# A transformer block on one core: the epsilon of both norms as a third triple of the statistics, negated means left out, and the waits of an instruction put in another order

## The chip, the cores and the metric

The kernel runs on one core of one Trainium2 chip. The metric is the device time of one execution in microseconds; of the kernel before, three runs took 204.25, 204.28 and 204.39 us, the median is 204.28 us. Lines such as L515 are lines of the kernel before, unless the text says otherwise.

## The reference

One layer: a norm, an attention with softmax feature maps and linear cost, a residual; then a second norm, a gated feed-forward part and a residual. S is 2048 rows, D 448, 16 heads of 28, F 1792, all in bf16.

```python
def _layernorm(x, axis=-1, eps=1e-5):
    m = jnp.mean(x, axis=axis, keepdims=True)
    v = jnp.var(x, axis=axis, keepdims=True)
    return (x - m) / jnp.sqrt(v + eps)

def _A_ref(x, wqkv, w_phi, wo):
    qkv = (x @ wqkv).reshape(B, S, 3, H, Dh).transpose(2, 0, 3, 1, 4)
    q, k, v = qkv[0], qkv[1], qkv[2]
    pq = jnp.einsum("bhsd,hdf->bhsf", q, w_phi)
    pk = jnp.einsum("bhsd,hdf->bhsf", k, w_phi)
    phi_q = jnp.concatenate([_softmax(pq), _softmax(-pq)], axis=-1)
    phi_k = jnp.concatenate([_softmax(pk), _softmax(-pk)], axis=-1)
    kv = jnp.einsum("bhsf,bhsd->bhfd", phi_k, v)
    z = jnp.einsum("bhsf->bhf", phi_k)
    num = jnp.einsum("bhqf,bhfd->bhqd", phi_q, kv)
    den = jnp.einsum("bhqf,bhf->bhq", phi_q, z)[..., None] + 1e-6
    return (num / den).transpose(0, 2, 1, 3).reshape(B, S, D) @ wo

h = x + _A_ref(_layernorm(x), A_wqkv, A_w_phi, A_wo)
ln = _layernorm(h)
h2 = h + (sigmoid(ln @ w_gate) * (ln @ w_up)) @ w_down
```

## The kernel before

The 2048 rows are 16 tiles of 128 rows, each a row of `x_sb` with 448 columns. Every piece of work is an operation with a name, such as `xn3` (the normalised rows of tile 3) or `kva5`. A table at the head of the file, `ORDER`, gives for each of the five engines the names in the order in which that engine runs them; for some operations it also decides on which engine they run, where the code offers two or three. The class `Graph` takes the operations with what they read and write, finds from that which must wait for which, and emits for every engine its queue with the waits. An engine runs its queue in order, so an instruction that waits holds back all behind it.

**The first norm.** For each tile `stats` records `bst` (`bn_stats`, six numbers a row: two triples of count, mean and sum of squared deviations) and `agg` (`bn_aggr`, which makes mean and variance of the triples, into `mv1`), both on VectorE. For groups of tiles (0, 1, 2 and 3 alone, 4-5, 6-7, 8 to 11, 12 to 15) `rstd` then records four operations, named after the first tile of the group: `ve1` adds epsilon to the variance (L522), `pow1` raises it to -1/2 on GpSimd (L527, into `rst1`), `nm1` negates the mean (L525), and `nb1` multiplies the negated mean by `rst1` (L531, from tile 2 on). `xnorm` makes the normalised tile `xn`: on ScalarE as scale times x plus bias (`rst1` and `nb1`, L540), on VectorE or GpSimd as (x + nm1) times rst1 (L543). There are three buffers for these tiles, so `xn7` can start when the transpose of tile 4 has read its buffer.

**From the normalised tile to the features.** Tiles 0 to 3 are transposed on TensorE (`xT0` to `xT3`, L507) and copied to `xnT` on ScalarE or VectorE (`xT0e` and so on, L500); from tile 4 on the transposes `xT` are DMAs from the SP queue, in order, with the load of the last two tiles of x (`x14`) between `xT5` and `xT6`. TensorE multiplies with the folded weights for k and phi (`pp` for two tiles, `pva`/`pvb` for one) and with those for v (`vv`, or the same pair). All matmuls of this kind work on 64 rows at a time, in two halves that run side by side and share line L305. ScalarE takes the exponentials of both signs (`ek`, L641 and L642), VectorE sums them (`ss`, L645) and takes the reciprocal (`rs`, L651), GpSimd or VectorE multiplies the two (`phi`, L655), and TensorE adds each tile to the sums over all rows with `kvb` and `kva`, whose operand is `phi` and v. Between these run the products for q (`pqa`, `pqb`), whose exponentials `eq` (L691) ScalarE takes.

**The second part.** `num` multiplies the features of q with the sums; VectorE forms `rsm`, `qq`, `b`, `c` and `rden` per tile (L768 to L776; the first two tiles share `rsm0` and `qq0`, L740 and L741), `o` is the attention's output (L780), `wo` the projection. For tiles 0 and 1 the residual is added by TensorE itself, and the second norm takes `bs2` (L799) and `ag2` (L802) from the result; `ve0` and `ve1` (L803) add epsilon, `pow2` (L817) raises, `hn` (L821) normalises with the mean as it stands. All other tiles of the second norm use sums of squares by ScalarE (`sq`) and keep their own `ve`. Then `ga`, `gb` (gate and up), `sig` (L881), `hh` (L882), `dn`/`dp`/`dm` (down), `fin` (L916) and the stores.

**The waits.** For each operation `emit` gathers what it has to wait for in `o.waits`, at most one entry per engine and one per DMA, sorted by the number under which the producer was recorded, highest first. The queue then issues one wait after another in that order. In the built program the last of them belongs to the instruction that follows; each earlier one, sometimes two together, is an instruction of its own.

Of the kernel before, what the change touches and what calls it, by code (L numbers as in the profile page):

```python
# [6 lines left out]
ALU = mybir.AluOpType  # L7
# [3 lines left out]
ENGINES = ("sp", "act", "pe", "dve", "pool")  # L11
# [7 lines left out]
class Graph:  # L19
# [86 lines left out]
    def emit(self, nc):  # L106
        ops = self.ops
        self.schedule()
        queues = {e: [] for e in ENGINES}
        for i in self.order:  # L110
            o = ops[i]
            o.pos = len(queues[o.eng])
            queues[o.eng].append(o)
        known = {e: {} for e in ENGINES}
        for i in self.order:
            o = ops[i]
            kn = known[o.eng]
            todo = []
            for j, raw in o.deps.items():
                p = ops[j]  # L120
                if self.needs_wait(p, o, raw):
                    key, v = (("d",) + p.sem, p.val) if p.dma is not None else (("e", p.eng), p.pos + 1)
                    todo.append((key, v, j))
            todo.sort(key=lambda t: -t[2])
            o.waits = []
            for key, v, j in todo:
                if kn.get(key, 0) >= v:
                    continue
                o.waits.append(j)
# [58 lines left out]
P = 128  # L188
D = 448
# [10 lines left out]
EPS = 1e-5  # L200
# [57 lines left out]
    ),  # L258
    "dve": (
# [16 lines left out]
    ),  # L276
    "pool": (
# [5 lines left out]
    ),  # L283
# [38 lines left out]
def build(nc, A_x, A_wqkv, A_w_phi, A_wo, B_w_gate, B_w_up, B_w_down, out):  # L322
    S = A_x.shape[1]
    assert A_x.shape[0] == 1 and A_x.shape[2] == D and S == 2048
    NT = S // P
# [7 lines left out]
    with ExitStack() as es:  # L333
        def sb(name, shape, d=dt.bfloat16):
            return es.enter_context(nc.sbuf_tensor(name, shape, d))
        f32 = dt.float32
# [2 lines left out]
        neghalf = sb("neghalf", [P, 4], f32)  # L339
        mask2 = sb("mask2", [P, 2], f32)  # L340
        par = sb("par", [P, 2])
        st2 = sb("st2", [P, 2, 6], f32)
        mv2 = sb("mv2", [P, 2, 2], f32)
        x_sb = sb("x_sb", [P, NT, D])
        h_sb = x_sb
        st1 = sb("st1", [P, NT, 6], f32)
        mv1 = sb("mv1", [P, NT, 2], f32)
        ve1 = sb("ve1", [P, NT], f32)
        rst1 = sb("rst1", [P, NT], f32)
        nb1 = sb("nb1", [P, NT], f32)  # L350
        nm1 = sb("nm1", [P, NT], f32)
        sum2 = sb("sum2", [P, NT], f32)
        nm2 = sb("nm2", [P, NT], f32)
        ssq2 = sb("ssq2", [P, NT], f32)
# [37 lines left out]
        def bk(i):  # L392
            return psum[:, i * 512:(i + 1) * 512]
# [9 lines left out]
        def B(i):  # L403
            return ("bank", i)

        def load(name, dst, src, w, kb, r=(), eng="sp"):
# [8 lines left out]
                                                      base=0, pattern=[[-1, P]], channel_multiplier=1),  # L415
           r=["ident"], w=["ident"])
        op("pool", "neghalf", lambda e: e.memset(neghalf[:], -0.5), w=["neghalf"])
        def epsl0(e):
            e.memset(epsl[:, 0:64], EPL)
            return e.memset(epsl[:, 64:P], 0.0)  # L420
# [90 lines left out]


        def stats(t):
            op("dve", "bst%d" % t, lambda e: e.bn_stats(st1[:, t, :], x_sb[:, t, :]), r=[("x", t)], w=[("st1", t)])  # L514
            op("dve", "agg%d" % t, lambda e: e.bn_aggr(mv1[:, t, :], st1[:, t, :]), r=[("st1", t)], w=[("mv1", t)])  # L515

        def rstd(ts):
            a, b = ts[0], ts[-1] + 1
            n = b - a

            def fve(e):
                return e.tensor_scalar(ve1[:, a:b], mv1[:, a:b, 1], EPS, None, op0=ALU.add)  # L522

            def fnm(e):
                return e.tensor_scalar(nm1[:, a:b], mv1[:, a:b, 0], -1.0, None, op0=ALU.mult)  # L525
            op(("dve", "pool"), "ve1_%d" % a, fve, r=[("mv1", t) for t in ts], w=[("ve1", a)])
            op("pool", "pow1_%d" % a, lambda e: e.tensor_tensor(rst1[:, a:b], ve1[:, a:b], neghalf[:, 0:n], ALU.pow),  # L527
               r=[("ve1", a), "neghalf"], w=[("rst1", a)])
            op(("dve", "pool"), "nm1_%d" % a, fnm, r=[("mv1", t) for t in ts], w=[("nm1", a)])
            if a >= 2:  # L530
                op("pool", "nb1_%d" % a, lambda e: e.tensor_tensor(nb1[:, a:b], nm1[:, a:b], rst1[:, a:b], ALU.mult),  # L531
                   r=[("nm1", a), ("rst1", a)], w=[("nb1", a)])

        def xnorm(t, a):
            s = t % NX
            src = windows(x_sb[:, t, :])
            dst = xn_pad[:, s, :].rearrange("p (a f) -> p a f", a=2)

            def fa(e):
                return e.activation(dst, src, ACT.Identity, bias=nb1[:, t:t + 1], scale=rst1[:, t:t + 1])  # L540

            def fd(e):
                return e.tensor_scalar(dst, src, nm1[:, t:t + 1], rst1[:, t:t + 1], op0=ALU.add, op1=ALU.mult)  # L543
            r = [("x", t), ("nm1", a), ("rst1", a)]
            if a < 2:
                op(("dve", "pool"), "xn%d" % t, fd, r=r, w=[("xn", s)])
            else:
                op(("act", "dve", "pool"), "xn%d" % t, (fa, fd, fd), r=r + [("nb1", a)], w=[("xn", s)])
            if t < 4:
                pe_transpose("xT%d" % t, [xn_pad[:, s, kt * P:(kt + 1) * P] for kt in range(KT)], 6 + t % 2,  # L550
                             xnT[0][:, :, TS(t)], ("xn", s), ("xnT", t))
            else:
                op("sp", "xT%d" % t, lambda e: e.dma_start_transpose(out=xnT[t // 4][:, :, TS(t)], in_=xn_pad[:, s, :]),
                   r=[("xn", s)], w=[("xnT", t)], dma="tr", nring=64)
# [241 lines left out]
        def resid(t, b, ha=False):  # L796
            c, s = t // 4, t % NH
            if ha:
                st = op("dve", "bs2_%d" % t, lambda e: e.bn_stats(st2[:, t % 2, :], bk(b)[:, 0:D]), r=[B(b)], w=[("st2", t)])  # L799
                op(("act", "dve"), "h%d" % t, (lambda e: e.copy(h_sb[:, t, :], bk(b)[:, 0:D]),  # L800
                                               lambda e: e.tensor_copy(h_sb[:, t, :], bk(b)[:, 0:D])), r=[B(b)], w=[("x", t)], after=[st])
                op("dve", "ag2_%d" % t, lambda e: e.bn_aggr(mv2[:, t % 2, :], st2[:, t % 2, :]), r=[("st2", t)], w=[("mv2", t)])  # L802
                op(("dve", "pool"), "ve%d" % t, lambda e: e.tensor_scalar(ve2[:, t:t + 1], mv2[:, t % 2, 1:2], 1.0, EPS, op0=ALU.mult,  # L803
                                                                          op1=ALU.add), r=[("mv2", t)], w=[("ve2", t)])
            else:
                op("dve", "h%d" % t, lambda e: e.scalar_tensor_tensor(out=h_sb[:, t, :], in0=bk(b)[:, 0:D], scalar=1.0, in1=x_sb[:, t, :],  # L806
                                                                      op0=ALU.mult, op1=ALU.add, accum_out=sum2[:, t:t + 1]),
                   r=[B(b), ("x", t)], w=[("x", t), ("sum2", t)])
            if not ha:
# [7 lines left out]
            op("pool", "pow2_%d" % t, lambda e: e.tensor_tensor(rst2[:, t:t + 1], ve2[:, t:t + 1], neghalf[:, 0:1], ALU.pow),  # L817
               r=[("ve2", t), "neghalf"], w=[("rst2", t)])
# [169 lines left out]
```

## Time and profile before

The profile is of one execution on the chip.

| what | value |
|---|---|
| median of three runs | 204.28 us |
| span of the profiled execution | 202.8 us |
| PE (matmuls) busy | 195.9 us, 97% of the span |
| VectorE (DVE) busy | 135.5 us, 67% |
| ScalarE (ACT) busy | 95.7 us, 47% |
| GpSimd (POOL) busy | 55.6 us, 27% |
| bn_aggr, L515, 16 times | 161 ns mean |
| ve1 / nm1 of one tile on POOL, L522 / L525 | 218 / 234 ns mean |
| pow1 of 1, 2 and 4 tiles, L527 | 571, 707 and 1006 ns mean |
| granted TensorE clock | 1.00 in every stage |

The time of a run is longer than the span, since it holds what lies before the first and behind the last instruction that the profile counts. Rows of the timeline give the start, the length, the engine and line, and in brackets how long the engine was idle before and what ended that. Busy times of PE are modelled ends of pipelined matmuls. An engine's share of the whole span is a mean over stages with different limits.

### The profile page before, as it was taken

What the parts mean: (1) busy time and instruction counts of PE and PEld (TensorE: products, weight loads), DVE (VectorE), ACT (ScalarE), POOL (GpSimd) and SP (SyncE); (2) the same over time, 40 slices, a digit from 0 to 9 for tenths busy, and PEclk for the clock granted to TensorE, in tenths of its full rate; (3) what the DMA queues carried; (4) which work ended last, traced back from release to release, by engine and by line L of the source; (5) the groups of instructions that cost most, each with busy time, mean ns of one, the idle gap of its engine ahead of it and who ended that gap; (6) DMA issues with size and microseconds to landing.
All of it is one profiled execution on the core that took longest, in us unless ns stands there. A gap on an engine that the chain in (4) does not pass through costs nothing.

```text
span 202.8 us, 5881 instructions
## 1 busy us (share of the span) xinstructions
PE 195.9 (97%) x2508; PEld 109.4 (54%) x2508; DVE 135.5 (67%) x328; ACT 95.7 (47%) x191; POOL 55.6 (27%) x97
## 2 busy tenths in 40 slices
PE   7889999999979999999999999999999999999995
PEld 3734556665448776677444444444554555454443
DVE  5899999979998897858667967536432422272224
ACT  3887989988882527222333342324422212222220
POOL 5599699723144303700033020001400000000000
DMA  6985516849949411251004411030212000004003
GB/s 154 316 141 123 80 33 89 230 158 279 308 37 229 55 31 29 50 82 26 3 3 100 100 29 26 3 74 24 58 47 54 0 0 3 0 3 136 0 0 94
DMA packets 32867, 16.27 MB, mean 80 GB/s; under 512 B 25096, under 2 KB 31944, under 8 KB 32840
## 3 DMA queue, kind: packets, MB, share of 16 engines
q1 hardware_dynamic: 32336, 15.86, 34.9%
q8 instruction: 20, 0.33, 0.7%
q10 hardware_dynamic: 504, 0.03, 0.2%
q14 instruction: 7, 0.06, 0.1%
HBM read 8.34 MB, written 1.84 MB: 50 GB/s over the span
## 4 chain that ended last, share of the span: by engine, by line
PE 84%; DVE 8%; POOL 2%; DMA 2%; issue 1%; SPq 1%; ACT 0%; DVEq 0%
PE psum L305 78%; PE psum L909 5%; DVE st L514 2%; DMA x_sb<-in_A_x_dram 2%; DVE ss L645 2%; POOL o_pad L780 1%; DVE b_sb L771 1%; DVE xn_pad L543 1%; SPq L407 1%; DVE c_sb L774 1%; PE psum L507 0%; POOL xn_pad L543 0%; DVE rs L651 0%; DVE xnT L500 0%; POOL rst L527 0%
## 5 line engine op out<-in xcount | busy, mean ns | idle before, releaser
L305 PE MATMUL psum<-xnT,wg_sb 64*128 64x512 bf16 (+1 forms) x490 | 93.1, 334 | 0.3 <-DVE rden L776 0.2
L305 PE MATMUL psum<-xnT,wu_sb 64*128 64x512 bf16 (+1 forms) x490 | 92.9, 334 | 0.0
L881 ACT ACTIVATE sg_sb<-psum 128x512 bf16<-128x512 f32 (+1 forms) x70 | 34.8, 511 | 91.4 <-PE psum L305 90.9
L882 DVE SCALAR_TENSOR_TENSOR hhT<-sg_sb,psum 128x512 bf16<-128x512 bf16 (+1 forms) x70 | 38.9, 576 | 53.3 <-ACT sg_sb L881 53.0
L305 PEld LDWEIGHTS psum<-xnT,wg_sb 64*128 64x128 bf16 x490 | 44.4, 94 | 23.4 <-DVE hhT L882 4.8
L305 PEld LDWEIGHTS psum<-xnT,wu_sb 64*128 64x128 bf16 x490 | 44.4, 94 | 13.5
L305 PE MATMUL psum<-wd_sb,hhT 64*128 64x448 bf16 x336 | 36.8, 350 | 0.0
L305 PEld LDWEIGHTS psum<-wd_sb,hhT 64*128 64x128 bf16 x336 | 16.9, 94 | 15.1 <-DVE x_sb L806 0.5
L305 PE MATMUL psum<-Wk,xnT 64*128 64x448 bf16 x112 | 22.1, 351 | 0.3 <-ACT Wk L500 0.2
L305 PE MATMUL psum<-wv_sb,xnT 64*128 64x448 bf16 x112 | 22.2, 351 | 0.1
L815 POOL TENSOR_SCALAR ve<-ssq 128x1 f32<-128x1 f32 x11 | 2.6, 233 | 57.8 <-ACT junk L812 57.5
L655 POOL TENSOR_TENSOR phi<-hhT,rs 128x896 bf16<-128x896 bf16 x10 | 17.3, 1749 | 3.6 <-DVE ve L522 1.8
L645 DVE TENSOR_REDUCE ss<-hhT 128x32 f32<-128x896 bf16 x16 | 16.9, 1063 | 0.3 <-ACT hhT L642 0.3
L691 ACT ACTIVATE eq<-psum 120x1024 bf16<-120x1024 f32 x16 | 15.7, 1028 | 1.3 <-PE psum L305 1.1
L305 PE MATMUL psum<-xnT,Wq 64*120 64x512 bf16 x112 | 15.0, 385 | 0.1
L305 PE MATMUL psum<-wo_o,oT 64*128 64x448 bf16 x56 | 13.2, 350 | 0.0
L305 PE MATMUL psum<-wo_e,oT 64*128 64x448 bf16 x56 | 13.2, 349 | 0.0
L916 DVE SCALAR_TENSOR_TENSOR x_sb<-psum,x_sb 128x448 bf16<-128x448 f32 (+2 forms) x17 | 9.4, 591 | 2.7 <-PE psum L909 1.6
L909 PE MATMUL psum<-wd_sb,hhT 128*128 128x448 bf16 (+2 forms) x70 | 11.2, 316 | 0.0
L305 PEld LDWEIGHTS psum<-Wk,xnT 64*128 64x128 bf16 x112 | 7.8, 94 | 6.1 <-PE psum L305 0.5
L780 POOL TENSOR_TENSOR o_pad<-c_sb,rden 128x448 bf16<-128x448 bf16 x8 | 7.4, 935 | 11.1 <-DVE rden L776 11.0
L771 DVE TENSOR_TENSOR b_sb<-psum,qq 128x464 bf16<-128x464 f32 x16 | 10.2, 638 | 0.3
(99 smaller groups left out, 236.9 us busy)
## 6 DMA issues: line engine op xcount, KB each, us to landing
out_dram<-x_sb SPq DMA_DIRECT2D x15, 112.0 KB, 1.8
x_sb<-in_A_x_dram SPq DMA_DIRECT2D x7, 224.0 KB, 4.6
wd_sb<-in_B_w_down_dram SPq DMA_DIRECT2D x7, 224.0 KB, 4.4
wg_sb<-in_B_w_gate_dram SPq DMA_DIRECT2D x3, 448.0 KB, 5.5
wu_sb<-in_B_w_up_dram SPq DMA_DIRECT2D x3, 448.0 KB, 5.9
wv_sb<-in_A_wqkv_dram SPq DMA_DIRECT2D x2, 224.0 KB, 4.9
wk_sb<-in_A_wqkv_dram SPq DMA_DIRECT2D x2, 196.0 KB, 3.8
wo_e<-in_A_wo_dram SPq DMA_DIRECT2D x1, 336.0 KB, 3.2
```

Of the source, the lines that this page charges most:

```text
L305: p = e.matmul(o, lhsT=w, rhs=r, start=st, stop=sp, tile_position=(row, 0))
L514: op("dve", "bst%d" % t, lambda e: e.bn_stats(st1[:, t, :], x_sb[:, t, :]), r=[("x", t)], w=[("st1", t)])
L645: op("dve", "ss%d" % t, lambda e: e.tensor_reduce(ss[:, s, :].rearrange("p (b h) -> p b h", h=2), eks.rearrange("p b (d h) -> p b h d", h= ...
L655: return e.tensor_tensor(phi[:, sp, :, :, :].rearrange("p b a n -> p (b a) n")[:, :, 0:56].rearrange("p b (d h) -> p b d h", h=2), eks.rea ...
L691: op("act", "eq%d_%d%s" % (c, i, "pm"[sg]), lambda e, sg=sg: e.activation(eq[c][:, sg, 2 * i:2 * i + 2, :].rearrange("p g n -> p (g n)"), ...
L771: op("dve", "b%d" % t, lambda e: e.tensor_tensor(h3(b_sb), OMv[:, :, :, 0:EV], h2(qq)[:, :, :, None].to_broadcast([P, NB, 8, EV]), ALU.mul ...
L780: return e.tensor_tensor(o_pad[:, t % NO, off:off + D].rearrange("p (h d) -> p h d", h=H), c_sb[:, t % NS, :, 0:DH], rden[:, t % NS, :][:, ...
L815: op(("pool", "dve"), "ve%d" % t, lambda e: e.tensor_scalar(ve2[:, t:t + 1], ssq2[:, t:t + 1], 1.0 / D ** 3, EPS, op0=ALU.mult, op1=ALU.ad ...
L881: op("act", "sig" + nm, lambda e: e.activation(sg_sb[:, k, 0:N], bk(bg)[:, 0:N], ACT.Tanh, scale=0.5), r=[B(bg)], w=[("sg", k)])
L882: op("dve", "hh" + nm, lambda e: e.scalar_tensor_tensor(out=hhT[(t0 // 4) % NHH][:, ff, ns], in0=sg_sb[:, k, 0:N], scalar=1.0, in1=bk(bu)[ ...
L909: p = e.matmul(bk(b)[:, lo:hi], lhsT=hb[:, ff, TS(t)], rhs=wd_sb[:, ff, lo:hi], start=ff == 0, stop=ff == FT - 1)
L916: op("dve", "fin%d%s" % (t, nm), lambda e: e.scalar_tensor_tensor(out=h_sb[:, t, lo:hi], in0=bk(b)[:, lo:hi], scalar=0.5, in1=h_sb[:, t, l ...
```

## The change

The statistics tiles `st1` and `st2` get nine columns for six. Columns 6 to 8 are a third triple with count 0, mean 0 and sum D times epsilon, written once by a new operation `steps` (four memsets on VectorE). `bn_stats` writes the first six columns as before, `bn_aggr` reads all nine, and its variance comes out with epsilon in it. So `ve1` of all groups is left out, and `ve0`, `ve1` of the second norm's tiles 0 and 1; `pow1` and these two `pow2` read `mv1` and `mv2`.

The negated mean `nm1` is left out: VectorE and GpSimd subtract the mean from `mv1` in place of adding its negative. `nb1` becomes one operation for each tile that ScalarE normalises (3, 4, 6, 11, 12 and 15; five groups had one before), as mean times -1 times `rst1`.

In `emit` the waits of an operation are sorted anew: loads first, then by the place of the producer in the order that `schedule` found, the latest last. That order goes by dependencies and queues alone and contains no times.

The tables of the five engines are otherwise as before: the names that remain stand in the same order, and TensorE, ScalarE and SP keep theirs.

```diff
+        rank = {i: n for n, i in enumerate(self.order)}
...
             o.waits = [j for j in o.waits if ops[j].dma is not None or ops[j].pos == last[ops[j].eng]]
+            o.waits.sort(key=lambda j: (ops[j].dma != "in", rank[j]))
...
-        "zero bd0 mask2 bst1 agg1 ve1_1 bst0 agg0 nm1_0 xn1 xn0 bst2 agg2 bst3 agg3 bst4 bst5 wTe3 agg4 agg5 bst6 "
-        "bst7 agg6 agg7 bst10 ve1_6 agg10 nm1_6 bst8 bst11 bst9 agg8 xT3e agg11 agg9 xT2e nm1_8 ve1_8 ss0 ss1 rs0 "
-        "bst13 rs1 ss2 bst12 bst14 rs2 agg12 agg13 agg14 bst15 ss3 xn10 ss4 rs3 agg15 rs4 ve1_12 nm1_12 phi3 ss5 "
+        "zero bd0 steps mask2 bst1 agg1 bst0 agg0 xn1 xn0 bst2 agg2 bst3 agg3 bst4 bst5 wTe3 agg4 agg5 bst6 "
+        "bst7 agg6 agg7 bst10 agg10 bst8 bst11 bst9 agg8 xT3e agg11 agg9 xT2e ss0 ss1 rs0 "
+        "bst13 rs1 ss2 bst12 bst14 rs2 agg12 agg13 agg14 bst15 ss3 xn10 ss4 rs3 agg15 rs4 phi3 ss5 "
...
-        "neghalf ident0 ident phipad wqpad epsl0 epsr0 nm1_1 pow1_1 ve1_0 pow1_0 nm1_2 ve1_2 ve1_3 v1ones pow1_3 "
-        "nm1_3 pow1_2 nb1_3 ve1_4 nm1_4 pow1_4 nb1_4 opad0 nb1_2 xn2 pow1_6 xn5 nb1_6 pow1_8 nb1_8 xn7 phi0 phi1 "
-        "xn8 xn9 phi2 phi4 pow1_12 nb1_12 xn13 phi6 xn14 phi8 phi9 phi10 phi11 phi13 o0 o1 ve0 pow2_0 o3 ve1 "
+        "neghalf ident0 ident phipad wqpad epsl0 epsr0 pow1_1 pow1_0 v1ones pow1_3 "
+        "pow1_2 nb1_3 pow1_4 nb1_4 opad0 xn2 pow1_6 xn5 nb1_6 pow1_8 nb1_11 xn7 phi0 phi1 "
+        "xn8 xn9 phi2 phi4 pow1_12 nb1_12 nb1_15 xn13 phi6 xn14 phi8 phi9 phi10 phi11 phi13 o0 o1 pow2_0 o3 "
...
+        def steps(e):
+            for st in (st1, st2):
+                e.memset(st[:, :, 6:8], 0.0)
+                p = e.memset(st[:, :, 8:9], D * EPS)
+            return p
+        op(("dve", "pool"), "steps", steps, w=["steps"])
...
-            op("dve", "bst%d" % t, lambda e: e.bn_stats(st1[:, t, :], x_sb[:, t, :]), r=[("x", t)], w=[("st1", t)])
-            op("dve", "agg%d" % t, lambda e: e.bn_aggr(mv1[:, t, :], st1[:, t, :]), r=[("st1", t)], w=[("mv1", t)])
+            op("dve", "bst%d" % t, lambda e: e.bn_stats(st1[:, t, 0:6], x_sb[:, t, :]), r=[("x", t)], w=[("st1", t)])
+            op("dve", "agg%d" % t, lambda e: e.bn_aggr(mv1[:, t, :], st1[:, t, :]), r=[("st1", t), "steps"], w=[("mv1", t)])
...
-            def fve(e):
-                return e.tensor_scalar(ve1[:, a:b], mv1[:, a:b, 1], EPS, None, op0=ALU.add)
-
-            def fnm(e):
-                return e.tensor_scalar(nm1[:, a:b], mv1[:, a:b, 0], -1.0, None, op0=ALU.mult)
...
-            op("pool", "pow1_%d" % a, lambda e: e.tensor_tensor(rst1[:, a:b], ve1[:, a:b], neghalf[:, 0:n], ALU.pow),
+            op("pool", "pow1_%d" % a, lambda e: e.tensor_tensor(rst1[:, a:b], mv1[:, a:b, 1], neghalf[:, 0:n], ALU.pow),
...
-                return e.tensor_scalar(dst, src, nm1[:, t:t + 1], rst1[:, t:t + 1], op0=ALU.add, op1=ALU.mult)
+                return e.tensor_scalar(dst, src, mv1[:, t, 0:1], rst1[:, t:t + 1], op0=ALU.subtract, op1=ALU.mult)
...
+            on_act = Graph.engine("xn%d" % t) == "act"
+            if on_act:
+                op(("pool", "dve"), "nb1_%d" % t, lambda e: e.tensor_scalar(nb1[:, t:t + 1], mv1[:, t, 0:1], -1.0, rst1[:, t:t + 1],
+                                                                            op0=ALU.mult, op1=ALU.mult),
+                   r=r[1:], w=[("nb1", t)])
...
-                op(("dve", "pool"), "ve%d" % t, lambda e: e.tensor_scalar(ve2[:, t:t + 1], mv2[:, t % 2, 1:2], 1.0, EPS, op0=ALU.mult,
-                                                                          op1=ALU.add), r=[("mv2", t)], w=[("ve2", t)])
+                op("pool", "pow2_%d" % t, lambda e: e.tensor_tensor(rst2[:, t:t + 1], mv2[:, t % 2, 1:2], neghalf[:, 0:1], ALU.pow),
+                   r=[("mv2", t), "neghalf"], w=[("rst2", t)])
```

More of the change, by code (lines that the diff above doesn't have):

```diff
@@ L69, in crosses, with engine @@
     @staticmethod
+    def engine(name):
+        return next(e for e in ENGINES if name in ORDER[e].split())
+    @staticmethod
     def crosses(p, o):
@@ L341, in build @@
         par = sb("par", [P, 2])
-        st2 = sb("st2", [P, 2, 6], f32)
+        st2 = sb("st2", [P, 2, 9], f32)
         mv2 = sb("mv2", [P, 2, 2], f32)
@@ L345, in build @@
         h_sb = x_sb
-        st1 = sb("st1", [P, NT, 6], f32)
+        st1 = sb("st1", [P, NT, 9], f32)
         mv1 = sb("mv1", [P, NT, 2], f32)
-        ve1 = sb("ve1", [P, NT], f32)
         rst1 = sb("rst1", [P, NT], f32)
         nb1 = sb("nb1", [P, NT], f32)
-        nm1 = sb("nm1", [P, NT], f32)
         sum2 = sb("sum2", [P, NT], f32)
@@ L519, in rstd @@
             n = b - a
-            def fve(e):
-                return e.tensor_scalar(ve1[:, a:b], mv1[:, a:b, 1], EPS, None, op0=ALU.add)
-            def fnm(e):
-                return e.tensor_scalar(nm1[:, a:b], mv1[:, a:b, 0], -1.0, None, op0=ALU.mult)
-            op(("dve", "pool"), "ve1_%d" % a, fve, r=[("mv1", t) for t in ts], w=[("ve1", a)])
-            op("pool", "pow1_%d" % a, lambda e: e.tensor_tensor(rst1[:, a:b], ve1[:, a:b], neghalf[:, 0:n], ALU.pow),
[L528 to L532, printed above, removed]
+            op("pool", "pow1_%d" % a, lambda e: e.tensor_tensor(rst1[:, a:b], mv1[:, a:b, 1], neghalf[:, 0:n], ALU.pow),
+               r=[("mv1", t) for t in ts] + ["neghalf"], w=[("rst1", a)])
         def xnorm(t, a):
@@ L542, in fd @@
             def fd(e):
[L543 to L548, printed above, removed]
+                return e.tensor_scalar(dst, src, mv1[:, t, 0:1], rst1[:, t:t + 1], op0=ALU.subtract, op1=ALU.mult)
+            r = [("x", t), ("mv1", t), ("rst1", a)]
+            on_act = Graph.engine("xn%d" % t) == "act"
[3 more added lines that the diff above has]
+                   r=r[1:], w=[("nb1", t)])
+            op(("act", "dve", "pool"), "xn%d" % t, (fa, fd, fd), r=[("x", t), ("rst1", a), ("nb1", t)] if on_act else r, w=[("xn", s)])
             if t < 4:
@@ L798, in resid @@
             if ha:
-                st = op("dve", "bs2_%d" % t, lambda e: e.bn_stats(st2[:, t % 2, :], bk(b)[:, 0:D]), r=[B(b)], w=[("st2", t)])
+                st = op("dve", "bs2_%d" % t, lambda e: e.bn_stats(st2[:, t % 2, 0:6], bk(b)[:, 0:D]), r=[B(b)], w=[("st2", t)])
                 op(("act", "dve"), "h%d" % t, (lambda e: e.copy(h_sb[:, t, :], bk(b)[:, 0:D]),
                                                lambda e: e.tensor_copy(h_sb[:, t, :], bk(b)[:, 0:D])), r=[B(b)], w=[("x", t)], after=[st])
-                op("dve", "ag2_%d" % t, lambda e: e.bn_aggr(mv2[:, t % 2, :], st2[:, t % 2, :]), r=[("st2", t)], w=[("mv2", t)])
-                op(("dve", "pool"), "ve%d" % t, lambda e: e.tensor_scalar(ve2[:, t:t + 1], mv2[:, t % 2, 1:2], 1.0, EPS, op0=ALU.mult,
-                                                                          op1=ALU.add), r=[("mv2", t)], w=[("ve2", t)])
+                op("dve", "ag2_%d" % t, lambda e: e.bn_aggr(mv2[:, t % 2, :], st2[:, t % 2, :]), r=[("st2", t), "steps"], w=[("mv2", t)])
+                op("pool", "pow2_%d" % t, lambda e: e.tensor_tensor(rst2[:, t:t + 1], mv2[:, t % 2, 1:2], neghalf[:, 0:1], ALU.pow),
+                   r=[("mv2", t), "neghalf"], w=[("rst2", t)])
             else:
@@ L816, in resid @@
                    r=[("ssq2", t)], w=[("ve2", t)])
-            op("pool", "pow2_%d" % t, lambda e: e.tensor_tensor(rst2[:, t:t + 1], ve2[:, t:t + 1], neghalf[:, 0:1], ALU.pow),
-               r=[("ve2", t), "neghalf"], w=[("rst2", t)])
+                op("pool", "pow2_%d" % t, lambda e: e.tensor_tensor(rst2[:, t:t + 1], ve2[:, t:t + 1], neghalf[:, 0:1], ALU.pow),
+                   r=[("ve2", t), "neghalf"], w=[("rst2", t)])
             def hnf(e):
```

## The prediction, made before the changed kernel ran

> **What bounds the kernel now.** I read the shares by engine first, then the table by stage, then the chain of work that ended last, and last the timeline of the first 26 us. The shares and the table by stage (stage start:end and length in us; busy us and instructions of PE, PEld, DVE, ACT, POOL; granted clock; DMA share; GB/s):
>
> ```profile
> PE 195.9 (97%) x2508; PEld 109.4 (54%) x2508; DVE 135.5 (67%) x328; ACT 95.7 (47%) x191; POOL 55.6 (27%) x97
> ```
>
> ```profile
> 12.84:16.50 3.66, 3.53 (x36) 1.54 (x38) 3.66 (x12) 3.00 (x7) 3.49 (x6) 1.00 0.69 74
> 16.50:21.00 4.50, 4.43 (x54) 2.08 (x50) 4.25 (x12) 3.90 (x11) 4.38 (x4) 1.00 0.49 109
> 21.00:25.45 4.45, 4.14 (x78) 2.36 (x77) 4.45 (x10) 4.42 (x12) 2.69 (x3) 1.00 0.60 91
> 25.45:35.00 9.55, 9.55 (x174) 5.57 (x176) 9.45 (x16) 8.58 (x19) 9.07 (x8) 1.00 0.40 59
> ...
> 60.60:100.00 39.40, 39.36 (x656) 28.34 (x658) 31.28 (x96) 15.15 (x43) 10.12 (x17) 1.00 0.37 66
> ```
>
> TensorE sets the end: from 25.45 us on it hardly pauses (9.55 of 9.55 us, then 39.36 of 39.40), so whatever it gains before 25.45 us is carried to the end, and nothing that the change takes from other engines later can help except at a pause of PE. The pauses are early. The chain that ended last shows where (start us, us, what):
>
> ```profile
> 12.01 0.78 POOL xn_pad L543
> 12.79 0.05 issue
> 12.84 0.40 PE psum L507 x4
> ...
> 17.52 1.09 DVE ss L645
> ...
> 21.58 1.67 DVE xn_pad L543
> 23.25 0.99 DVE ss L645
> ...
> 24.78 0.02 DVE ve L522
> 24.80 0.07 DVE nm L525
> 24.87 0.54 DVE phi L655
> 25.41 0.05 issue
> 25.45 19.21 PE psum L305 x360
> ```
>
> PE waits for xn2 of POOL, later VectorE is the chain, and PE waits for phi3. The timeline of 13.8 to 25.5 us gives the rest (start, us, engine, line, what, idle before):
>
> ```profile
> 13.84 0.39 DVE L525 TENSOR_SCALAR nm<-mv 128x4 f32<-128x4 f32 x1
> 14.14 0.16 DVE L522 TENSOR_SCALAR ve<-mv 128x4 f32<-128x4 f32 x1
> 14.21 2.07 DVE L645 TENSOR_REDUCE ss<-hhT 128x32 f32<-128x896 bf16 x2
> 16.62 3.33 POOL L655 TENSOR_TENSOR phi<-hhT,rs 128x896 bf16<-128x896 bf16 x2 [0.21 <-DVE rs L651]
> 21.41 1.69 POOL L655 TENSOR_TENSOR phi<-hhT,rs 128x896 bf16<-128x896 bf16 x1
> 21.50 1.75 DVE L543 TENSOR_SCALAR xn_pad<-x_sb,nm,rst 128x512 bf16<-128x512 bf16 x1
> 25.45 0.29 PE L305 MATMUL psum<-v,phi 64*128 64x58 bf16 x8 [0.32 <-DVE phi L655]
> ```
>
> xn10 takes 1.75 us where xn1 and xn0 took 0.40 and 0.41: it starts 0.09 us after phi2 on POOL and ends 0.15 us after it. So POOL's row phi0, phi1, xn8, xn9, phi2 dates VectorE, and phi0 (16.62) waits for rs0 on VectorE (0.21 us idle).
>
> By the Trainium skill, page "SBUF — State Buffer", section "Who interferes with whom", one SBUF port pair is shared by VectorE's two-port modes and GpSimd, and whichever starts first keeps it for its whole instruction; these two rows agree (1.75 against 0.40 us).
>
> **The change part by part.** *Removed before xn2.* POOL loses eight small operations at L522 and L525 between 3.7 and 10.6 us (0.21 to 0.24 us each) and the two-tile nb becomes one per ScalarE tile (three-operand, priced like L525, 0.23 against 0.20). Recomputed: pow1_3 can start 0.08 us after agg3 (7.95), at 8.03 instead of 8.33; pow1_2 8.6; nb1_3 9.3; pow1_4 waits for agg5 (9.44) and runs 9.5 to 10.2; nb1_4 to 10.5; opad0 to 10.8; xn2 10.9 to 11.6, not 12.0 to 12.8. PE isn't there then: xT3 starts at 12.21 and, as vva0 follows xT2 by 0.32 us, PE is free at 12.53. xT2 moves from 12.84 to 12.53: **0.31 us** for PE. The 0.4 us that xn1 and xn0 gain is worth nothing: VectorE then waits for x2 (6.38) and PE for the second half of wk (7.20), loads that don't move. Nor does ppa0 (10.46), which ends a row of ScalarE copies from 8.08 on.
>
> *Removed on VectorE.* ve1_6 and nm1_6 cost 0.07 us of start (bst8 11.40 becomes 11.33, behind agg10). nm1_8 and ve1_8 stand between xT2e and ss0: ss0 started 0.68 us after xT2e, and an instruction behind such a copy starts 0.31 us after it (nm1_8 did), so 0.37 us. Together ss0 at 13.77; its input ek0 was ready at 13.30, and ss1's (ek1, 14.17) doesn't hold it. So rs0, phi0 and POOL's row move by **0.44 us**, if xn7 lets phi0: POOL's shorter row gives pow1_8 by 15.1, nb1_11 by 15.3, xn7 by 16.1. xn10 then ends at 22.81 (ss2 to ss3 stay ahead: ss2 waits for ek2, which follows PE's 0.31). ve1_12 and nm1_12 before phi3 are gone too: between 0.05 (phi3 started 0.31 us behind rs4; agg15 started 0.26 behind rs3) and 0.09 (0.02 and 0.07 in the chain), taken 0.07. phi3 and with it kva3: 0.51 us earlier, 24.94. PE alone could be ready sooner: kvb2 starts at 24.86 and its eight occupy 0.13 (kva3 25.45, pvb7 behind it 25.58), so it is free at 24.99, less 0.31 is 24.68. The smaller gain counts: **-0.51**. phi4 of POOL, which kva4 meets closely (26.94 against 27.0), starts behind rs4 and is held by phi3 (2.08 against 1.69 us), so it moves along.
>
> *Added.* Four memsets (steps) on VectorE ahead of mask2: at most 0.15 us each (the 128x1 row of L522), 0.6 in all, between 1.35 and 2.84 us, where VectorE has 1.2 us idle until x1 lands; without that cover 0.6 us. The aggregation reads 9 columns, not 6 (0.161 us a piece at L515). No row has 9. Lower bound: nothing (the L522 rows of 1 and of 4 columns take 0.154 and 0.128). Upper bound: half again, +0.08, if the time goes by triples. I take 2 ns a column from 0.161 less 0.150 for five columns more, 6 ns, and with 14 of them ahead of phi3 **+0.08**. By the Trainium skill's page "VectorE: DVE Perf Modes", section "Side-by-side: where the cycles go for N=2048 bf16", plain mode does one element a cycle; 3 more would be some 3 ns, an estimate, and 0.04 for the 14; the sum below would be -0.53 by it. POOL has one nb more before xn13 (0.23 us), hidden: phi6 ends at 31.07, its matmuls come at 31.7.
>
> *Second norm.* ve0 and ve1 leave POOL (0.19 us each), so pow2_1 ends some 0.6 us earlier; but hn1 stands behind qq5, which waits for num5 of PE (57.63): **0**.
>
> *Waits re-sorted.* In the programs as built an instruction carries its last wait itself; each earlier one is an instruction of its own ahead of it. b0 had its wait for qq0 in front and now carries it: the chain shows 0.09 us from qq0's end (46.88) to b0 (46.97), against 0.03 at c0 (47.65, 0.03 behind b0): **-0.06**. The other way round, the twelve pva starts now have ScalarE's evacuation in front and the transpose last, which landed long before (one issued at 20.7 took 2.4 us, and its tile's pva8 starts after 25.9). What is queued behind is PE's whole row. It costs nothing while PE isn't waiting (9.55 of 9.55 busy); uncovered, I bound it by 0 and 0.06 each (0.05 from a release to PE's start, above). Taken: 0.
>
> Sum: -0.51 + 0.08 - 0.06 = **-0.49 us**. Span 202.8 becomes 202.3; what lies around it in the runs (their median 204.28 less 202.8, 1.48 us) stays: **203.79**, 0.24% under the median.
>
> **The rivals.** (1) *A transpose keeps its date.* xn7 needs the buffer that xT4 empties: issued 12.34, landed 3.2 us later, 15.54, and xn7 started at 15.64. If it lands no earlier (the stage from 10.46 to 12.84 has the DMA engines full), phi0 starts 16.4, gaining 0.22 for 0.44: 203.79 + 0.22 = 204.0. For: the share there; against: it is issued 0.4 us earlier. (2) *xn10 gets in first.* ss3 would end near 21.3 and xn10 start at 21.2, phi2 at 20.97: 0.23 us decide. Then VectorE saves up to 1.3 us more, and PE's own 0.77 (25.45 less 24.68) is the limit: 203.79 - 0.26 = 203.5. By the section of the Trainium skill named above the port goes to whoever starts first; this rival is that rule's other outcome. (3) *Aggregation by triples*, the other side: +0.08 each on L515, 14 ahead of phi3, 1.12 us of VectorE for my 0.08: 204.28 - 0.57 + 1.12 = 204.8. It decides from 0.04 us each (0.57 by 14). Against: a cost near that of one-column rows. (4) *The re-sorting bites*: 12 pva starts by 0.06, 0.72 us, if half of them do: 203.79 + 0.36 = 204.15; POOL's phi4, whose wait for rs4 now stands in front, would add one more 0.06. Against: PE's full stage.
>
> **How the numbers follow.** Forecast 0.50 (own range 203.55 to 203.95), (1) 0.18, (2) 0.12, (3) 0.12, (4) 0.08. 0.2% is 0.41 us, about what a measurement of this kernel can tell from no change; the forecast stands only 0.08 beyond it. Faster: 0.40 of the forecast's 0.50, all of (2), a little of (1): 0.55. Slower: (3) and a tail of (4) or unlucky port meetings: 0.15. No change: 0.30. The range goes from below (2), 203.2, into (3), 204.6.
>
> **What would show it.** In the changed profile: no row of ve at the first norm; xT2 without idle before it, near 12.5; ss0 near 13.8; phi0 near 16.2; xn10 still long and ending near 22.8; kva3 near 24.9; the aggregation under 0.17 us; b0 0.03 us behind qq0; PE still full from 25 to 44 us. An aggregation above 0.20 us, an xn10 of 0.4 us or idle PE before the pva rows would make it wrong.

## The result, and the profile after

The changed kernel takes 210.99 us (median of 6 runs, 210.49 to 211.72), the kernel before 204.26 us on the same chip (6 runs, 203.61 to 204.39). The ratio is 1.0343 with a 95% interval of 1.0317 to 1.0368: 3.4% slower, where 0.24% faster was forecast, and far outside the range of 203.2 to 204.6 us. The profiled execution's span went from 202.8 to 209.9 us.

The group rows of GpSimd's normalised tiles, one of before and one of after (line, engine, operation, tiles, shapes, count; busy us, mean ns of one; idle us before them):

```profile
L543 POOL TENSOR_SCALAR xn_pad<-x_sb,nm,rst 128x512 bf16<-128x512 bf16 x7 | 5.6, 809 | 0.2
```

```profile
L545 POOL TENSOR_SCALAR xn_pad<-x_sb,mv,rst 128x512 bf16<-128x512 bf16 x7 | 15.1, 2161 | 0.0
```

Same seven tiles, same shape, same engine; only the operands and the first operation differ. One row went from 0.81 to 2.16 us, seven of them from 5.6 to 15.1 us. GpSimd as a whole rose from 55.6 to 63.1 us, 30% of the span, which on the page looks harmless. The chain of waits of after shows why it isn't (start us, us, what):

```profile
10.56 2.08 POOL xn_pad L545
12.64 0.70 POOL rst L533
...
13.35 2.08 POOL xn_pad L545
...
17.03 2.06 POOL xn_pad L545
19.09 3.30 POOL phi L659 x2
22.39 2.24 POOL xn_pad L545 x2
24.63 2.44 issue
27.08 1.69 POOL phi L659
28.77 0.05 issue
28.82 22.91 PE psum L311 x355
```

From 10.56 to 28.77 us every step of the chain is GpSimd's ("issue" at 24.63 is the rest of the second of two xn rows: they ran from 22.37 for 4.74 us). Before, VectorE was the chain from 17.5 us on. In the queue, xn2, xn5 and xn7 stand ahead of phi0, and xn8 and xn9 ahead of phi2: phi0 moved from 16.62 to 19.05 us, phi2 from 21.41 to 27.08. The matmuls of kva2 need phi2. The timeline of TensorE there:

```profile
25.08 0.28 PE L311 MATMUL psum<-v,phi 64*128 64x58 bf16 x8
28.82 0.37 PE L311 MATMUL psum<-v,phi 64*128 64x58 bf16 x8 [3.46 <-POOL phi L659]
29.01 0.55 PE L311 MATMUL psum<-Wk,xnT 64*128 64x448 bf16 x1
```

TensorE stood for 3.46 us, and the matmuls behind the pause took 0.55 us where the same form takes 0.35 just ahead of it (24.89 us). The table by stage of after gives the reason (start:end, length; busy us and instructions of PE, PEld, DVE, ACT, POOL; granted clock; DMA share; GB/s):

```profile
12.84:25.45 12.61, 11.15 (x138) 5.18 (x136) 10.56 (x25) 9.67 (x25) 12.50 (x10) 1.00 0.34 64
25.45:35.00 9.55, 6.18 (x70) 3.11 (x72) 3.55 (x6) 4.22 (x9) 8.71 (x8) 0.64 0.34 57
28.82:34.00 5.18, 5.18 (x64) 2.70 (x66) 1.76 (x3) 1.77 (x5) 5.07 (x5) 0.50 0.30 58
```

The granted clock was 1.00 in all of these stages before; behind the pause it is 0.50 for some 5 us. By the Trainium skill's page "TensorE: Matmul & The Clock Gate", section "What's actually happening", the clock goes to half after an idle window of about 3.4 us and comes back after a busy one; this trace agrees (3.46 us of pause, then 0.50, and 1.00 again by 35 us). Not every pause of this length is followed by it here: one of 3.51 us, shown below, was not.

From the first b_sb on (46.97 us before, 53.98 after, +7.01) the two executions run alike: the spans differ by 7.1 us. So the whole loss is made between 10 us and the first b_sb.

### The profile page after: what moved, and what is told of

Read it like the earlier page. It is cut to its first block, busy times and chain, and to the rows that moved or that the text cites. A ratio compares the mean times of both kernels' runs of the same rounds, so it can differ in the third digit from the quotient of the medians.

```text
span 209.9 us, 5864 instructions
## 1 busy us (share of the span) xinstructions
PE 198.7 (95%) x2508; PEld 112.2 (53%) x2508; DVE 134.4 (64%) x324; ACT 95.4 (45%) x191; POOL 63.1 (30%) x87
## 4 chain that ended last, share of the span: by engine, by line
PE 81%; POOL 9%; DVE 3%; DMA 2%; issue 2%; SPq 1%
PE psum L311 76%; PE psum L913 5%; POOL xn_pad L545 4%; POOL phi L659 2%; DMA x_sb<-in_A_x_dram 2%; POOL rst L533 1%; SPq L411 1%; POOL o_pad L784 1%; DVE b_sb L775 1%; DVE c_sb L778 1%; DVE st L526 1%; POOL nb L549 0%; DVE xnT L512 0%; DVE rden L780 0%; DVE hn_pad L825 0%
## 5 line engine op out<-in xcount | busy, mean ns | idle before, releaser
L311 PE MATMUL psum<-wv_sb,xnT 64*128 64x448 bf16 x112 | 24.4, 377 | 1.2 <-ACT v L512 1.1
L311 PEld LDWEIGHTS psum<-wd_sb,hhT 64*128 64x128 bf16 x336 | 17.6, 94 | 14.4 <-DVE x_sb L810 0.5
L311 PE MATMUL psum<-Wk,xnT 64*128 64x448 bf16 x112 | 24.3, 377 | 0.3 <-ACT Wk L512 0.2
L659 POOL TENSOR_TENSOR phi<-hhT,rs 128x896 bf16<-128x896 bf16 x10 | 16.7, 1687 | 3.0 <-DVE rs L655 2.6
L545 POOL TENSOR_SCALAR xn_pad<-x_sb,mv,rst 128x512 bf16<-128x512 bf16 x7 | 15.1, 2161 | 0.0
L311 PEld LDWEIGHTS psum<-Wk,xnT 64*128 64x128 bf16 x112 | 8.6, 100 | 6.8 <-issue 2.2
L645 ACT ACTIVATE hhT<-psum 128x448 bf16<-128x448 f32 x16 | 8.9, 558 | 6.4 <-PE psum L311 6.3
```

The lines of the kernel that those rows point to most:

```text
L311: p = e.matmul(o, lhsT=w, rhs=r, start=st, stop=sp, tile_position=(row, 0))
L545: return e.tensor_scalar(dst, src, mv1[:, t, 0:1], rst1[:, t:t + 1], op0=ALU.subtract, op1=ALU.mult)
L645: e.activation(ek[:, s, :, 0, :], src, ACT.Exp)
L659: return e.tensor_tensor(phi[:, sp, :, :, :].rearrange("p b a n -> p (b a) n")[:, :, 0:56].rearrange("p b (d h) -> p b d h", h=2), eks.rea ...
```

## The experiments

**Is it GpSimd's subtraction?** Two kernels, one in each direction. e1_add is the changed kernel with the old operation on GpSimd's seven tiles; e2_sub is the kernel before with the new one there and nothing else. The seven tiles then hold x plus the mean, not x minus it, so both kernels serve for their times alone.

```diff
 e1_add (changed kernel), GpSimd's tiles only
-  tensor_scalar(dst, src, mv1[:, t, 0:1], rst1[:, t:t + 1], op0=ALU.subtract, op1=ALU.mult)
+  tensor_scalar(dst, src, mv1[:, t, 0:1], rst1[:, t:t + 1], op0=ALU.add, op1=ALU.mult)
 e2_sub (kernel before), GpSimd's tiles only
-  tensor_scalar(dst, src, nm1[:, t:t + 1], rst1[:, t:t + 1], op0=ALU.add, op1=ALU.mult)
+  tensor_scalar(dst, src, nm1[:, t:t + 1], rst1[:, t:t + 1], op0=ALU.subtract, op1=ALU.mult)
```

> The changed kernel, but the seven tiles of the first norm that GpSimd normalises add the mean where they should subtract it (so these tiles hold wrong values); operands, order and waits are those of the changed kernel. Theory A (the operation subtract is what made GpSimd's rows 2.1 us long): these rows go back to 0.77-0.81 us and the time to what the prediction said, 203.6 to 204.1 us. Theory B (the mean read from the two-column tile mv1 in place of nm1 makes the row slow): the rows stay at 2.1 us and the time at 211 us. Theory C (GpSimd's rows meet VectorE's on the shared port in the new order): rows between, 1 to 2 us, differing from tile to tile.

> The kernel before, but the same seven tiles on GpSimd subtract nm1 where they should add it (so these tiles hold wrong values); nothing else is changed. Theory A: their rows take 2.1 us in place of 0.81 and the time rises to 210-212 us, the whole loss of the changed kernel from this one word. Theories B and C: rows 0.8 us, time 204.3 us.

Measured: e1_add 203.57 us, ratio to before 0.9955 (0.9938 to 0.9971); e2_sub 211.54 us, ratio 1.0354 (1.0321 to 1.0387). The group rows of the seven tiles, of e1_add and of e2_sub:

```profile
L548 POOL TENSOR_SCALAR xn_pad<-x_sb,mv,rst 128x512 bf16<-128x512 bf16 x7 | 5.3, 765 | 0.9 <-PE psum L519 0.8
```

```profile
L546 POOL TENSOR_SCALAR xn_pad<-x_sb,nm,rst 128x512 bf16<-128x512 bf16 x7 | 15.2, 2173 | 0.2
```

One word in one operation makes the whole loss, and with add in its place the change is a gain of about 0.45%. The columns read (the mean out of a two-column tile, or nm) make no difference: e1_add's rows are fast reading from `mv1`, and e2_sub's are slow reading `nm1`.

**Which pairs of operations are slow?** Three kernels gave GpSimd's seven tiles different operations, each tile one, everything else as before.

```diff
 e3_pairs: tile 2 subtract-mult, 5 add-mult, 7 mult-add, 8 mult-subtract, 9 subtract-add,
           13 add-subtract, 14 add-add (columns nm1 and rst1)
 e8_pairs2: tile 2 mult-mult, 5 subtract alone, 7 add alone, 13 mult alone,
            14 subtract-mult with constants, 8 and 9 add-mult
 e12_pairs3: tile 2 mult alone, 14 mult alone by a constant, 5 subtract-mult and 13 add-mult
             with constants, 7 max-mult, 8 and 9 add-mult
```

> The kernel before, but each of the seven tiles on GpSimd takes another pair of operations with the same two pointers (values of these tiles are wrong): tile 2 subtract-mult, 5 add-mult, 7 mult-add, 8 mult-subtract, 9 subtract-add, 13 add-subtract, 14 add-add. Theory A as it stands: rows of 2.1 us wherever a subtract is in the pair (tiles 2, 8, 9, 13) and 0.77 elsewhere. Variant A': only pairs of a short list are fast (add-mult, perhaps mult-add), all others 2.1 us, so 14 is slow too. Theories B and C: 0.8 us everywhere.

> The kernel before with another operation on five of POOL's seven xn tiles, to measure each by itself: tile 2 multiply then multiply, tile 5 subtract alone, tile 7 add alone, tile 13 multiply alone, tile 14 subtract then multiply with constants in place of columns; tiles 8 and 9 keep add then multiply. Theory A' (only one add with one multiply, or a single operation, is fast): tile 2 at 2.1 us, tile 14 at 2.1, tiles 7 and 13 at 0.8 or less; tile 5 tells whether the subtraction alone is slow (2.1) or the pair (0.8). Rival (an add or a multiply by itself is fast, whatever it is joined with): add with add in e3_pairs already took 2.08, so this one falls if tile 2 is at 2.1 as well. The five tiles hold other values than the reference's.

> The kernel before with other operations on five of POOL's tiles, those that e8_pairs2 left open: tile 2 multiply alone by a column, tile 14 multiply alone by a constant, tile 5 subtract then multiply by constants, tile 13 add then multiply by constants, tile 7 maximum then multiply by columns. By what e3 and e8 have shown (fast: add-multiply, multiply-add, multiply-multiply; slow: every pair with a subtraction, add-add, and single operations at 1.58), tiles 2 and 14 take 1.6 us (e8's 2.01 for one multiply would then be another engine's doing), tile 5 takes 1.9 to 2.1, tile 7 2.1. Tile 13 tells whether constants are as fast as columns (0.77) or slow for themselves (1.9 or more). The five tiles hold other values than the reference's.

The rows of GpSimd in the timeline of e3_pairs (tiles 2, 5, 7, then 8 and 9 together, 13, 14):

```profile
11.66 2.09 POOL L548 TENSOR_SCALAR xn_pad<-x_sb,nm,rst 128x512 bf16<-128x512 bf16 x1
14.44 0.77 POOL L548 TENSOR_SCALAR xn_pad<-x_sb,nm,rst 128x512 bf16<-128x512 bf16 x1
16.64 0.77 POOL L548 TENSOR_SCALAR xn_pad<-x_sb,nm,rst 128x512 bf16<-128x512 bf16 x1
20.94 4.20 POOL L548 TENSOR_SCALAR xn_pad<-x_sb,nm,rst 128x512 bf16<-128x512 bf16 x2
29.95 2.09 POOL L548 TENSOR_SCALAR xn_pad<-x_sb,nm,rst 128x512 bf16<-128x512 bf16 x1
33.68 2.08 POOL L548 TENSOR_SCALAR xn_pad<-x_sb,nm,rst 128x512 bf16<-128x512 bf16 x1
```

The same of e8_pairs2 (tiles 2, 5, 7, 13, 14) and of e12_pairs3 (tiles 2, 5, 7, 13, 14):

```profile
11.91 0.77 POOL L548 TENSOR_SCALAR xn_pad<-x_sb,nm,rst 128x512 bf16<-128x512 bf16 x1
...
13.37 1.58 POOL L550 TENSOR_SCALAR xn_pad<-x_sb,nm 128x512 bf16<-128x512 bf16 x1
...
16.34 1.58 POOL L550 TENSOR_SCALAR xn_pad<-x_sb,nm 128x512 bf16<-128x512 bf16 x1
...
28.03 2.01 POOL L550 TENSOR_SCALAR xn_pad<-x_sb,nm 128x512 bf16<-128x512 bf16 x1
...
31.67 1.94 POOL L552 TENSOR_SCALAR xn_pad<-x_sb 128x512 bf16<-128x512 bf16 x1
```

```profile
11.78 1.58 POOL L548 TENSOR_SCALAR xn_pad<-x_sb,nm 128x512 bf16<-128x512 bf16 x1
...
14.03 1.96 POOL L550 TENSOR_SCALAR xn_pad<-x_sb 128x512 bf16<-128x512 bf16 x1
...
17.40 2.09 POOL L552 TENSOR_SCALAR xn_pad<-x_sb,nm,rst 128x512 bf16<-128x512 bf16 x1
...
29.70 0.62 POOL L550 TENSOR_SCALAR xn_pad<-x_sb 128x512 bf16<-128x512 bf16 x1
...
33.76 1.51 POOL L548 TENSOR_SCALAR xn_pad<-x_sb 128x512 bf16<-128x512 bf16 x1
```

Put together, a 128x512 bf16 row of GpSimd takes:

| operations | us |
|---|---|
| add-mult, mult-add, mult-mult, columns | 0.77 |
| add-mult, constants | 0.62 |
| subtract-mult, mult-subtract, subtract-add, add-subtract, add-add, max-mult, columns | 2.08 to 2.12 |
| subtract-mult, constants | 1.94, 1.96 |
| add alone, subtract alone, one column | 1.58 |
| mult alone, one column | 1.58, 2.01 |
| mult alone, one constant | 1.51 |

So it isn't the subtraction as such: add-add is as slow. (The row of two at 20.94 us holds tiles 8 and 9; the four rows from there to 33.68 take between 2.078 and 2.124 us each.) Of nine pairs tried on columns three are fast, the ones made of multiplies and adds with at least one multiply. Two of the expectations for e8_pairs2 fell: multiply-multiply is fast, and a single operation is not, it takes twice the time of the fast pair. Why one multiply took 2.01 us in e8_pairs2 (28.03 us) and 1.58 in e12_pairs3 was not tested. The traces point to a meeting with VectorE: in e8_pairs2 its phi5 row had started just ahead of the multiply,

```profile
27.97 0.62 DVE L665 TENSOR_TENSOR phi<-hhT,rs 128x896 bf16<-128x896 bf16 x1
```

and in the kernel before, where the same two rows met (phi5 at 28.16 us, xn13 at 28.35), the fast pair took 1.06 us for 0.77.

**How much of the loss is the clock?** e4_fill is the changed kernel with 15 matmuls of zeros in TensorE's queue ahead of kva2, so that the pause is filled while GpSimd's rows stay slow.

```diff
-  ... pvb6 kvb1 kva2 pva7 ...
+  ... pvb6 kvb1 fill kva2 pva7 ...
+        def fill(e):
+            for _ in range(15):
+                p = e.matmul(bk(4)[:, 0:512], lhsT=zero[:, 0:P], rhs=zero[:, 0:512], start=True, stop=True)
+            return p
```

> The changed kernel with 15 matmuls of 512 columns on zeros put on TensorE just ahead of kva2, in the 3.46 us in which it waited for phi2; they are 3.2 us at full clock and write a bank that is free there. Theory D (about half of the 7.1 us is the TensorE clock, which stood at 0.50 from 29 to 33 us behind that wait, and not GpSimd's rows themselves): the granted clock stays at 1.00, the stretch from kva2 to the sums of q shrinks from 22.9 us towards 19.2, and the time falls by 2 to 3.7 us, to 207.3-209. Rival (GpSimd's later long rows would have held TensorE in that stretch anyway): clock 1.00, but the time stays within 1 us of 211, with idle time of TensorE on phi4, phi6 or phi8.

Measured: 209.76 us, ratio 1.0265 (1.0249 to 1.0280), against the changed kernel's 1.0343. Its table by stage shows that the clock held while kva2 still started at 28.61 us:

```profile
25.45:28.61 3.16, 3.04 (x17) 1.19 (x14) 0.93 (x2) 1.83 (x4) 3.16 (x3) 1.00 0.43 73
28.61:34.00 5.39, 5.39 (x90) 3.23 (x92) 3.50 (x6) 3.04 (x7) 5.28 (x6) 1.00 0.30 59
```

In 5.39 us TensorE got 90 instructions done, where the changed kernel got 64 in 5.18. In the chain of waits of the changed kernel the last 48 matmuls ahead of rsm0 start at 51.78 us, in that of e4_fill at 49.72. So of the profiled execution's 7.1 us about 2 are the clock, and 5 are GpSimd's rows alone. The time fell by less than expected (209.76 us, where 207.3 to 209 stood): with the clock held, TensorE came to a later row of GpSimd before that was done and waited 0.76 us again, which it didn't in the changed kernel. So what the clock costs and what the rows cost don't simply add.

```profile
39.27 0.29 PE L311 MATMUL psum<-v,phi 64*128 64x58 bf16 x8 [0.76 <-POOL phi L659]
```

The runs say the same without the filling: the changed kernel's mean granted clock was 0.992 in three runs (spans 208.7, 208.7, 208.9 us) and 0.984 in three (209.4, 209.6, 209.9), 0.87 us for a step of 0.008; one step more would be 207.9 us (an estimate, 208.77 less 0.87), and e4_fill's four runs at full clock have spans of 207.8 to 208.3. e2_sub has the steps too: 209.1 us at 1.000, 209.6 and 209.8 at 0.992, 210.8 at 0.984. Its profiled execution is the one at 1.000, though its pause was 3.51 us:

```profile
26.04 0.28 PE L305 MATMUL psum<-v,phi 64*128 64x58 bf16 x8
29.83 0.29 PE L305 MATMUL psum<-v,phi 64*128 64x58 bf16 x8 [3.51 <-POOL phi L658]
29.95 0.35 PE L305 MATMUL psum<-Wk,xnT 64*128 64x448 bf16 x1
```

A pause of the same length thus costs nothing beside itself in one execution, and up to about 2 us more in another.

**What is the rest of the change worth, and which of its parts?** Six kernels. e5_muladd keeps the dropped negated means but lets GpSimd multiply and add (x times rst plus nb), for which seven more nb rows stand on GpSimd; e6_muladd_nosort is that without the sorting of the waits; e7_before_sort is the kernel before with the sorting alone; e9_triple the kernel before with the third triple in the first norm alone; e11_add_nosort is e1_add without the sorting; e10_keepnm takes all that helps: both triples, VectorE subtracting, negated means and nb by groups as before for the tiles of GpSimd and ScalarE, no sorting.

```diff
 e5_muladd, GpSimd's tiles
+  tensor_scalar(dst, src, rst1[:, t:t + 1], nb1[:, t:t + 1], op0=ALU.mult, op1=ALU.add)
 e6, e10, e11
-            o.waits.sort(key=lambda j: (ops[j].dma != "in", rank[j]))
 e7 (kernel before)
+            o.waits.sort(key=lambda j: (ops[j].dma != "in", rank[j]))
 e9 (kernel before)
-            op(("dve", "pool"), "ve1_%d" % a, fve, r=[("mv1", t) for t in ts], w=[("ve1", a)])
 e10, GpSimd's tiles
+  tensor_scalar(dst, src, nm1[:, t:t + 1], rst1[:, t:t + 1], op0=ALU.add, op1=ALU.mult)
```

> The changed kernel with POOL's seven tiles written x*rst + nb (multiply, then add) in place of (x - mean)*rst; nb is made for these tiles too, by seven more POOL rows of some 0.26 us. Theory A' (POOL is slow for every pair of operations but one add with one multiply): the seven rows go back to 0.77 to 0.81 us, POOL spends about 1.8 us more on nb than in e1_add (7 x 0.26), of which only nb1_2, nb1_5 and nb1_7, ahead of phi0, could be late (0.8 us on phi0, which had 1.1 us and more in hand before phi1's date matters): 203.4 to 204.3 us, correct values and no slower than the kernel before. Rival: the slow rows come from reading the mean out of the three-column statistics tile, not from the pair of operations: e1_add already speaks against it, and e5 reads no statistics in the POOL rows, so it would be fast by this rival too. Rival: the extra nb rows on POOL cost their full 1.8 us: 205.3.

> e5_muladd without the sorting of the waits, so that the third triple and the dropped negated means stand alone. If the sort costs and brings nothing: within 0.2% of e5_muladd. If the sort is where the 0.8 us of e1_add come from: e6 is at 204.0 to 204.8 and e5 at 203.4 to 204.0.

> The kernel before with the sorting of the waits alone. If the sort does nothing to the time: 204.3 us, ratio 0.998 to 1.002. If it is what e1_add gained by: 203.4 to 203.8.

> The kernel before with the third triple alone, in the first norm alone: the eight rows that added epsilon (ve) go, negated means, nb by groups, the second norm and the waits stay. What e1_add gained beside the subtraction comes to 0.49 us by the prediction (the ve rows, the negated means of tiles 0 and 1 and the second norm together). Theory: the ve rows are the most of it (two of 0.15 to 0.23 us on VectorE and POOL ahead of the second transpose), 203.9 to 204.3 us, ratio 0.997 to 0.999 to before. Rival: the gain is the negated means' and the triple is worth nothing by itself because bn_aggr is 12 ns longer: 204.5, ratio 0.9995 to 1.001.

> The changed kernel without the sorting, with the negated means kept for the groups from tile 2 on (as before: one row per group), so that POOL can add and nb is one row per group again; VectorE subtracts the mean in its three tiles; both norms have the triple. POOL's seven rows at 0.77 to 0.81 us. Theory (the e5 and e6 kernels lost most of e1_add's 0.8 us to their seven more nb rows on POOL): 203.5 to 204.0 us, ratio 0.995 to 0.998, faster than e6's 0.9988. Rival (what e1_add gained is the dropped negated means): at e6's ratio, 0.998 to 1.000.

> e1_add without the sorting of the waits (POOL's seven tiles add the mean in place of subtracting it). If the sort costs about 0.1%, as e5 against e6 and e7 against before have it: 203.3 to 203.7 us, ratio 0.993 to 0.996. If the sort was what e1_add gained by: 0.997 to 1.000.

| kernel | median us | before, same chip | ratio, 95% interval |
|---|---|---|---|
| e5_muladd | 204.41 | 204.51 | 0.9999 (0.9985 to 1.0013) |
| e6_muladd_nosort | 204.21 | 204.51 | 0.9988 (0.9977 to 0.9999) |
| e7_before_sort | 204.85 | 204.51 | 1.0013 (1.0002 to 1.0025) |
| e9_triple | 204.07 | 204.49 | 0.9983 (0.9968 to 0.9998) |
| e10_keepnm | 203.72 | 204.49 | 0.9971 (0.9955 to 0.9987) |
| e11_add_nosort | 203.69 | 204.49 | 0.9963 (0.9947 to 0.9979) |

With multiply and add, e5 has GpSimd's rows back at 0.77 us in most places, and loses nothing against before, but it gains nothing either (204.41 us, where 203.4 to 204.3 were expected). Its profile shows part of the reason: of its seven more nb rows of 0.26 us on GpSimd two stand between phi1 and phi2; phi2 starts at 22.43 us (20.88 in e1_add), and TensorE waits 0.63 us for it, until 24.18. The triple alone is worth 0.17%. Sorting the waits alone costs 0.13% on the kernel before; e5 against e6 points the same way, e1_add against e11 doesn't (0.9955 and 0.9963, on different chips), so it is a cost of 0 to 0.25% whose place wasn't found. e10_keepnm beats both kernels of the case: 0.29% faster than before, 3.6% faster than the change as made (0.9971 by 1.0343). Its interval overlaps e9's; that the second triple and VectorE's subtraction add anything to the triple of the first norm isn't shown.

## Why the prediction was wrong

**The step that failed** stands in the paragraph "Removed before xn2" as "xn2 10.9 to 11.6", and in "Removed on VectorE" as "xn7 by 16.1": the changed xn row on GpSimd was given the duration of the row of before at L543. The edit from adding the negated mean to subtracting the mean isn't in the sum at all, with no price, no bound and no rival. The row measured 2.08 us and more, for seven rows 9.5 us more of GpSimd, and that took 7.1 us of the span where 0.5 were to be gained. No row of GpSimd in the trace of before showed a subtraction, and the nearest rows don't reach the measured time: its add-multiply takes 0.77 us for 512 columns, its phi rows, another form, 1.69 for 896, which makes 0.97 for 512 (an estimate). What could have been said is that the price was unknown. The prediction bounded a few ns of an aggregation from both sides, and left a changed operation on seven tiles of a serial queue unbounded.

**The other steps**, read in e1_add, where only that operation is back:

- *The second transpose.* In e1_add the chain shows it behind the first without a gap (eight transposes from 12.23 us, 0.55 us); forecast 12.53. Right. In the changed kernel it waited 0.43 us for the slow xn2.
- *ss0 at 13.77, phi0 at 16.2.* Measured 13.55 and 16.08 in e1_add: the right way, the gain larger than forecast (0.66 us for 0.44 at ss0, 0.54 for 0.44 at phi0). In the changed kernel ss0 came at 13.48, and phi0 at 19.05.
- *xn10 blocked and ending at 22.81.* In e1_add it took 1.65 us and ended at 22.71, right. The rival "xn10 gets in first" also occurs: in e10_keepnm, with phi2 behind it at 20.61, it took 0.40, and in the changed kernel too (22.27 us, ahead of xn8), one of the signs that the prediction named against itself. The rows of e1_add and e10_keepnm:

```profile
21.06 1.65 DVE L545 TENSOR_SCALAR xn_pad<-x_sb,mv,rst 128x512 bf16<-128x512 bf16 x1
```

```profile
20.45 0.40 DVE L551 TENSOR_SCALAR xn_pad<-x_sb,mv,rst 128x512 bf16<-128x512 bf16 x1
```

- VectorE thus pays nothing for the subtraction: 0.40 us in e10_keepnm, as the adding rows of before. Giving the new operation no price of its own was right there; for GpSimd the same was done without a row of GpSimd's.
- *The aggregation.* 173 ns for 161, so 12 ns each and 0.17 us on 14, where 6 and 0.08 were taken; inside the bounds. The rival by triples (+80 ns) is out.
- *The nb row.* 264 ns on GpSimd, 230 forecast; hidden where the change put it; with seven more of them (e5) TensorE waited for phi2.
- *The four memsets* took 0.06 to 0.09 us each on VectorE, ahead of 0.99 us of idle time: hidden, right.
- *b0.* 0.03 us behind the end of qq0 in the changed kernel (53.95 and 53.98), 0.09 before: right. But the sorting as a whole costs up to 0.25% on the kernel before (e7), so "taken: 0" for the other waits was too kind; the fourth rival's direction is borne out there.
- *The sum of -0.49.* e1_add's b_sb starts at 46.42 us for 46.97, -0.55; its ratio makes it -0.6 to -1.3 us of 204.3. The sign is right, and the size right or too small. The path below it came out only in part. pvb7, behind kva3, starts at 24.90 us in e1_add for 25.58, a gain of 0.68 where 0.51 were forecast, and TensorE waits 0.15 us for ScalarE at 29.54, where it was to stay full until 44 us. In e11_add_nosort the first rival occurs: xn7 waits 0.88 us for a transpose, and phi0 starts at 16.72, later than in the kernel before. Yet phi3 starts there at 23.15 for 24.78, since xn10 took 0.81 us for 1.75, and the kernel is about as fast as e1_add. So the date of phi0 alone didn't carry the gain; how xn10 meets GpSimd's rows weighs more than the forecast gave it, and that e1_add came so near to the sum is in part luck.

The prediction's list of what would prove it wrong had "idle PE before the pva rows"; TensorE was idle before kva2, with pva7 behind it, for the unpriced reason.

## What to carry to other kernels

A changed operation code is a new instruction: where the trace has no row of that operation on that engine, its price is unknown, however equal the arithmetic and however little the other engine minds. Before simplifying an expression on GpSimd, look which pair of operations it becomes; here a multiply joined with an add or another multiply is the form to keep, even if it costs one small row for a negated operand, and even an add, a subtraction or a multiply alone was slower than the pair. An engine busy for 30% of the span can still be the bound of a stage if its queue is serial and the next engine's first input stands at its end.

## What the runs showed of the hardware that was not expected

- GpSimd's time for one 128x512 bf16 row depends on the pair of operations by a factor of 2.7 (0.77 against 2.08 us); VectorE took 0.40 us for add-multiply and for subtract-multiply alike. By the Trainium skill's page "GPSIMD Engine Reference", section "Elementwise — side-by-side cycle accounting", a best case of 512 elements is measured at 769 ns; the three fast pairs on columns agree (0.77 us). Add-multiply with constants took less (0.62) and every other operation tried here more, and the measurement decides.
- Fewer operations can be slower: multiply alone takes 1.58 us, multiply then multiply 0.77.
- A pause of TensorE of about 3.5 us costs its own length, and nine of the ten executions of the changed kernel and e2_sub also show a mean granted clock below 1.00, with spans some 0.5 to 2 us longer than at full clock (from 207.9, the estimate above, and 209.1); filling the pause with matmuls of zeros kept the clock at 1.00 in all four runs and gave 2 us of the profiled execution back.
